# Scores of six head pairs from 64-row operands on the two row halves of TensorE, with the high parts of q and k rounded on ScalarE

## The chip, the cores and the metric

The kernel runs on one core of one Trainium2 chip. A core has TensorE (matmuls; PE in the profile, and PEld for its weight loads), VectorE (DVE), ScalarE (ACT), GpSimd (POOL) and SyncE (SP), which here only issues transfers. The metric is the device time of one execution in microseconds (us). TensorE's granted clock has two levels, 1.2 and 2.4 GHz; the profile shows it as a share of 2.4.

## What is computed

Attention over 16 heads (2 batches of 8) with rotary embedding, then two dense blocks, all in float32:

```python
q_rot, k_rot = rotate(q), rotate(k)            # (2, 8, 576, 64)
scores = q_rot @ k_rot.T / sqrt(64)
attn = exp(scores - max(scores)); attn /= attn.sum(-1) + 1e-9
x = (attn @ v), heads side by side             # (1152, 512)
x = elu(x @ w_in) @ w_out                      # 512 -> 2048 -> 512
x = mish(x @ w2_in) @ w2_out                   # 512 -> 2048 -> 512
```

## The kernel before

Two heads of 64 dimensions make a pair: one head lies on rows (partitions) 0 to 63, the other on 64 to 127. There are eight pairs, p = 0 to 7, called the first to the eighth here. Each tensor that goes into a large product is split into a high part, rounded to the type fp32r that TensorE multiplies fast, and a low part, the rest; a product is the sum of high by high, low by high and high by low.

The work of a pair is cut into nine **units** (TPP = 9), and a hand-written loop over units u = 9 p + i fixes the order of everything on every engine. Units 0 to 7 of a pair are 128 queries of one head each; unit 8 is the 64 left-over queries of both heads together, with block-diagonal tiles bh and bl. In unit u the loop issues, in this order on TensorE: the **score block** of unit u (`do_S`, line 415, into the PSUM tile ps_s of 128 x 2 x 288, one 288-key half in each of its two banks), the **transposes** of the probabilities of unit u - 3 (`do_T`, lines 481 to 486, into psT and psL), and in some units products with v (`do_av`, line 521, into psA, 64 output columns each) or the small products that turn the sums (`do_spread`, lines 458 and 462). VectorE takes the maximum of a score block (mn, line 422), ScalarE the exponential (P, line 435); both move the transposed P out of psT (pt, lines 499 and 501). ScalarE also keeps R, the inverse sums, out of psA (line 466) and rounds the result to XH (line 548); GpSimd or VectorE subtract to get XL (line 552).

`prepare(p, k)` is called in unit k of pair p - 1. With k = 0 it splits k of pair p (`split_half`: GpSimd rounds kh, line 323, and subtracts kl, line 324), with k = 1 it splits q, with k = 2 to 7 GpSimd rotates the pair after that, one step a unit. Between them SyncE issues the transfers that lay the parts out for the score blocks (`stack_k`, `stack_q`). For the first two pairs (FLAT = 2) VectorE and ScalarE split, and nothing is laid out anew except bh and bl.

Two forms of score block stand in the kernel:

- First and second pair: two units at a time, one of each head. Each matmul contracts the 64 rows of its head, so twelve matmuls alternate between rows 0 to 63 and rows 64 to 127.
- Third to eighth pair: transfers stack kh over kl in ka (128 rows) and qh over qh in qa; qb holds ql over zeros. Two matmuls a key half, each on 128 rows, make the three products:

```python
work.append([
    (d["qa"][:, h, cols], lambda ks: d["ka"][:, h, ks]),
    (d["qb"][:, h, cols], lambda ks: d["ka"][:, h, ks]),
])
```

From the seventh pair on, weights of the first dense block are unpacked between the units (`weight_part`): steps of GpSimd and VectorE, then ScalarE's high part and GpSimd's low part. Behind the eighth pair the dense blocks follow.

Of the kernel before, what the change touches and what calls it, by code (L numbers as in the profile page):

```python
# [21 lines left out]
def plain(ap):  # L22
    return ap.bitcast(F32)
# [3 lines left out]
def kernel(  # L27
# [218 lines left out]
    def attention(att, ps, tail):  # L246
# [61 lines left out]
        def split_alloc(p):  # L308
            d = {}
            for nm in ("kh", "kl", "ql"):  # L310
                d[nm] = att.tile([128, S], F32R, tag=nm, name=nm, bufs=2)
            for nm in ("qa",) if p < FLAT else ("ka", "qa"):
                d[nm] = att.tile([128, 2, S], F32R, tag=nm, name=nm, bufs=2)
            d["qh"] = d["qa"][:, 0, :] if p < FLAT else att.tile([128, S], F32R, tag="qh", name="qh", bufs=1)
            i = p % 2
            d["qb"] = qb[i]
            d["bh"], d["bl"] = bd[i]
            sp_t[p] = d

        def split_half(p, i, h, l):  # L320
            d = sp_t[p]
            x = qk_t[p][:, i, :]
            nc.gpsimd.tensor_scalar(out=d[h], in0=x, scalar1=1.0, scalar2=0.0, op0=ALU.mult, op1=ALU.add)
            nc.gpsimd.tensor_tensor(out=d[l], in0=x, in1=plain(d[h]), op=ALU.subtract)
# [24 lines left out]

        def spread(dst, src, r):  # L350
            for h in range(2):
                nc.sync.dma_start(out=plain(dst[64 * r:64 * r + 64, h, :]), in_=plain(src[64 * h:64 * h + 64, :]))

        def stack_k(p):
            d = sp_t[p]
            spread(d["ka"], d["kh"], 0)
            spread(d["ka"], d["kl"], 1)

        def stack_q(p):
            d = sp_t[p]  # L360
            for r in range(0 if p < FLAT else 2):
                spread(d["qa"], d["qh"], r)
            if p >= FLAT:
                spread(d["qb"], d["ql"], 0)
            for r in range(2):
                sl = slice(64 * r, 64 * r + 64)
                nc.sync.dma_start(out=plain(d["bh"][sl, 64 * r:64 * r + 64]), in_=plain(d["qh"][sl, S - 64:S]))
                nc.sync.dma_start(out=plain(d["bl"][sl, 64 * r:64 * r + 64]), in_=plain(d["ql"][sl, S - 64:S]))
# [11 lines left out]
        def do_S(u):  # L380
# [4 lines left out]
            else:  # L385
                us = (u,)
            work = []
            for w in us:
                psS[w] = ps_s()
                if tiles[w % TPP] is None:  # L390
                    work.append([
                        (d["bh"], lambda ks: d["kh"][:, ks]),
                        (d["bh"], lambda ks: d["kl"][:, ks]),
                        (d["bl"], lambda ks: d["kh"][:, ks]),
                    ])
                    continue
                h, t = tiles[w % TPP]
                cols = slice(128 * t, 128 * t + 128)
                if p < FLAT:
                    rows = slice(64 * h, 64 * h + 64)  # L400
                    work.append([
                        (d["qh"][rows, cols], lambda ks, rows=rows: d["kh"][rows, ks]),
                        (d["ql"][rows, cols], lambda ks, rows=rows: d["kh"][rows, ks]),
                        (d["qh"][rows, cols], lambda ks, rows=rows: d["kl"][rows, ks]),
                    ])
                else:
                    work.append([
                        (d["qa"][:, h, cols], lambda ks: d["ka"][:, h, ks]),
                        (d["qb"][:, h, cols], lambda ks: d["ka"][:, h, ks]),
                    ])  # L410
            for a in range(len(work[0]) if work else 0):
                for j in range(2):
                    for w, passes in zip(us, work):
                        l, r = passes[a]
                        nc.tensor.matmul(  # L415
                            psS[w][:, j, :HS], lhsT=l, rhs=r(slice(j * HS, j * HS + HS)),
                            start=(a == 0), stop=(a == len(passes) - 1),
                        )

# [145 lines left out]
        for i in range(2):  # L565
# [5 lines left out]
            bd.append(pair)  # L571
        qb = [att.tile([128, 2, S], F32R, name=f"qb{i}") for i in range(2)]
        for t in sums:
            nc.vector.memset(t[:, :, 1:2], 1e-9)
        nc.vector.memset(pl_t[1][S - 512:128, 256:384], 0.0)
        for t in qb:
            nc.gpsimd.memset(plain(t[64:128]), 0.0)
        nc.gpsimd.memset(halves, 0.0)
# [63 lines left out]
        for u in range(max(av_at) + 1):  # L642
            p, i = divmod(u, TPP)
            for k in range(8):
                if p and i == k and p + 1 < NP:
                    prepare(p + 1, k)
            if u == 2:
# [75 lines left out]
            if u == 1:  # L723
                first_hi(*HEAD[-1])
                nc.scalar.activation(out=tab[:, 0:2, :], in_=tab[:, 2:4, :], func=AF.Copy, scale=QSCALE)
                rope_half(1, 0, nc.gpsimd)
            if u in (5, 6):
                second_split(2 if u == 5 else 0)
# [241 lines left out]
```

## Time and profile before

| | us |
|---|---|
| runs of the kernel: median (lowest to highest) | 559.64 (558.6 to 561.39) |
| profiled execution, first to last instruction | 559.2 |
| TensorE busy in it | 546.1 (98%) |
| VectorE, ScalarE, GpSimd busy | 375.8, 267.4, 244.4 |
| mean granted clock of TensorE, share of 2.4 GHz | 0.994 |

A matmul's row begins when it starts and ends when its results are written, so rows of matmuls that follow each other overlap: what one costs is the distance between starts, not its length. A group of the timeline (x4) reaches from the first start to the last end. What stands in brackets behind a row is the idle time of that engine before it and what ended it; "issue" means that the profile shows nothing that it waited for.

### The profile page before, as it was taken

To read this page: it belongs to the slowest core of one execution; us is meant where nothing else is said; L and a number is where in the kernel's file an instruction comes from. 1 tells how busy PE (TensorE), PEld (TensorE's weight loads), DVE (VectorE), ACT (ScalarE), POOL (GpSimd) and SP (SyncE) were. 2 spreads that over 40 slices of the span, in tenths; PEclk is the share of its full clock that TensorE was granted. 3 is DMA by queue.
4 is the path that set the end of the run, shared out by engine and by line. 5 is a ranking of instruction groups with operands and counts; after the bars stand their busy time and mean duration, and the time that the engine had idled before them with its cause. 6 is when DMAs were issued, how large, how long until landed. Compare 5 with 4: busy or idle time off the path is not lost.

```text
span 559.2 us, 8818 instructions
## 1 busy us (share of the span) xinstructions
PE 546.1 (98%) x3328; PEld 500.5 (90%) x3328; DVE 375.8 (67%) x560; ACT 267.4 (48%) x459; POOL 244.4 (44%) x227
## 2 busy tenths in 40 slices
PE   7889999999999999999999999999999999999997
PEld 6667878888898999999999999999989989989985
DVE  4868777879867888888889878857336555521221
ACT  3746666677656675554554556344342233132120
POOL 7979898953315434434334531534414433310000
PEclk9979999999999999999999999999999999999999
DMA  7379778764331333323232321423222131000012
GB/s 234 106 208 222 184 207 215 198 140 144 88 114 42 113 113 111 112 78 93 96 112 76 114 76 38 139 88 114 84 105 90 62 114 43 34 0 1 38 39 94
DMA packets 49258, 59.82 MB, mean 107 GB/s; under 512 B 20928, under 2 KB 39104, under 8 KB 48448
## 3 DMA queue, kind: packets, MB, share of 16 engines
q1 hardware_dynamic: 48672, 58.67, 35.6%
q8 instruction: 26, 0.43, 0.3%
q10 hardware_dynamic: 544, 0.59, 0.3%
q14 instruction: 16, 0.13, 0.1%
HBM read 47.51 MB, written 2.36 MB: 89 GB/s over the span
## 4 chain that ended last, share of the span: by engine, by line
PE 87%; DVE 3%; POOL 3%; issue 3%; DMA 2%; ACT 1%; SPq 0%; POOLq 0%; ACTq 0%
PE ps_s L187 33%; PE ps_h L801 18%; PE ps_g L777 17%; PE ps_s L415 7%; PE psA L521 7%; PE psT L481 4%; DMA qk_t<-in_qk_dram 1%; DVE mn L422 1%; DMA bh<-qa 1%; ACT P L435 1%; POOL wu L96 1%; POOL wo0bl L127 1%; POOL wo0l L127 1%; PE psL L486 0%; DVE wu L108 0%
## 5 line engine op out<-in xcount | busy, mean ns | idle before, releaser
L100 DVE TENSOR_SCALAR wu<-wu 128x512 int32<-128x512 int32 x64 | 39.7, 620 | 43.1 <-POOL wu L96 43.1
L759 ACT ACTIVATE ta<-ps_s 128x768 f32<-128x768 f32 x24 | 19.5, 812 | 100.8 <-PE ps_s L187 100.8
L422 DVE TENSOR_REDUCE mn<-ps_s 128x1 f32<-128x576 f32 x72 | 53.5, 752 | 21.0 <-PE ps_s L415 20.8
L435 ACT ACTIVATE P<-ps_s,mn 128x576 f32<-128x576 f32 x72 | 53.1, 740 | 14.7 <-DVE mn L422 14.3
L104 DVE SCALAR_TENSOR_TENSOR wu<-raw,wu 128x512 int32<-128x512 int32 x64 | 50.6, 791 | 2.0
L187 PE MATMUL ps_s<-XH,wi0h 128*128 128x384 f32 x192 | 49.1, 336 | 0.0
L108 DVE SCALAR_TENSOR_TENSOR wu<-raw,wu 128x512 int32<-128x512 int32 x64 | 47.8, 747 | 1.8
L187 PE MATMUL ps_s<-XL,wi1h 128*128 128x384 f32 x192 | 48.9, 335 | 0.0
L187 PE MATMUL ps_s<-XL,wi0h 128*128 128x384 f32 x192 | 48.8, 335 | 0.0
L187 PE MATMUL ps_s<-XH,wi1l 128*128 128x384 f32 x192 | 48.8, 335 | 0.0
L187 PE MATMUL ps_s<-XH,wi0l 128*128 128x384 f32 x192 | 48.8, 335 | 0.0
L187 PE MATMUL ps_s<-XH,wi1h 128*128 128x384 f32 x192 | 48.7, 334 | 0.0
L96 POOL TENSOR_SCALAR wu<-raw 128x512 f32<-128x512 f32 x64 | 46.4, 728 | 4.3
L127 POOL TENSOR_TENSOR wi0l<-wu,wi0h 128x512 fp32r<-128x512 f32 x16 | 23.0, 1440 | 57.5 <-ACT wi0h L126 57.5
L127 POOL TENSOR_TENSOR wi1l<-wu,wi1h 128x512 fp32r<-128x512 f32 x16 | 24.3, 1523 | 54.1 <-ACT wi1h L126 54.1
L127 POOL TENSOR_TENSOR wo1l<-wu,wo1h 128x512 fp32r<-128x512 f32 x16 | 23.3, 1462 | 48.6 <-ACT wo1h L126 48.6
L481 PE MATMUL psT<-idn,P 128*128 128x128 f32 x288 | 43.7, 276 | 0.0
L761 DVE TENSOR_TENSOR g<-ta,g 128x768 fp32r<-128x768 f32 x16 | 17.5, 1093 | 37.0 <-ACT g L760 37.0
L501 ACT ACTIVATE pt<-psT 128x512 f32<-128x512 f32 x44 | 26.2, 597 | 28.9 <-PE psT L481 28.9
L521 PE MATMUL psA<-pt,v_t 128*64 128x256 f32 (+1 forms) x240 | 37.1, 410 | 2.3 <-DVE pt L499 1.8
L481 PEld LDWEIGHTS psT<-idn,P 128*128 128x128 f32 x288 | 35.2, 143 | 2.0 <-issue 1.4
L187 PEld LDWEIGHTS ps_s<-XH,wi0h 128*128 128x128 f32 x192 | 34.7, 188 | 1.4 <-issue 0.8
(177 smaller groups left out, 1370.1 us busy)
## 6 DMA issues: line engine op xcount, KB each, us to landing
raw<-in_w_in_dram SPq DMA_DIRECT2D x32, 512.0 KB, 3.7
raw<-in_w_out_dram SPq DMA_DIRECT2D x32, 512.0 KB, 3.2
qk_t<-in_qk_dram SPq DMA_DIRECT2D x6, 1152.0 KB, 5.5
qa<-qh SPq DMA_DIRECT2D x24, 144.0 KB, 2.7
out_dram<-Y SPq DMA_DIRECT2D x9, 256.0 KB, 2.0
ka<-kh SPq DMA_DIRECT2D x12, 144.0 KB, 3.1
ka<-kl SPq DMA_DIRECT2D x12, 144.0 KB, 3.0
qb<-ql SPq DMA_DIRECT2D x12, 144.0 KB, 2.7
```

Of the source, the lines that this page charges most:

```text
L96: nc.gpsimd.tensor_scalar(out=u, in0=high.bitcast(F32), scalar1=REBASE, scalar2=0.0, op0=ALU.mult, op1=ALU.add)
L100: nc.vector.tensor_scalar(out=ui, in0=ui, scalar1=3, scalar2=0x7FFFFFF8, op0=ALU.logical_shift_left, op1=ALU.bitwise_and)
L104: nc.vector.scalar_tensor_tensor(out=ui, in0=high, scalar=-0x80000000, in1=ui, op0=ALU.bitwise_and, op1=ALU.bitwise_or)
L108: nc.vector.scalar_tensor_tensor(out=ui, in0=low, scalar=29, in1=ui, op0=ALU.logical_shift_right, op1=ALU.bitwise_or)
L127: nc.gpsimd.tensor_tensor(out=lo, in0=u, in1=plain(hi), op=ALU.subtract)
L187: nc.tensor.matmul(o[:, j, :CH], lhsT=ws[j][i][:, cc, :], rhs=x[:, cc, t * CH:t * CH + CH], start=(k == 0), stop=(k == 3 * NC - 1),)
L422: nc.vector.tensor_reduce(out=m, in_=psS[u][:, :, :HS], axis=AX.XY, op=ALU.min)
L435: nc.scalar.activation(out=P.rearrange("p (j n) -> p j n", j=2), in_=psS.pop(u)[:, :, :HS], func=AF.Exp, scale=-1.0, bias=mn_t.pop(u), acc ...
L481: nc.tensor.transpose(tv[:, c, :], P[:, k:k + 128], idn)
L521: nc.tensor.matmul(o[64 * h:64 * h + 64, cols], lhsT=v, rhs=rhs, start=(c == 0 and first), stop=(c == 4), skip_group_check=True,)
L777: nc.tensor.matmul(o[:, j, :CH], lhsT=WO[f][w][:, e * 128:e * 128 + 128], rhs=g_part(f, t, i), start=(k == 0), stop=(k == 3 * GF - 1),)
L801: nc.tensor.matmul(o, lhsT=l, rhs=w, start=(k == 0), stop=(k == 3 * GF - 1))
```

## The change

For the third to eighth pair the tiles ka, qa and qb are gone. kx and qx hold the swapped halves: the rows of one head moved to the other half of the partitions, for kx only the half of the keys that is needed there. A score block is now six matmuls on 64 rows: the three products for the first key half from rows 0 to 63, and those for the second from rows 64 to 127, in turn. Of each head one key half comes from the untouched tiles (`native`), the other from kx and qx (`swapped`). The rounding of kh and qh of these pairs moves from GpSimd to ScalarE, and `prepare` moves from the start of a unit to a place behind the unit's exponential. The two clearings of qb at the start fall away.

```diff
         def split_alloc(p):
             d = {}
-            for nm in ("kh", "kl", "ql"):
+            for nm in ("kh", "kl", "qh", "ql"):
                 d[nm] = att.tile([128, S], F32R, tag=nm, name=nm, bufs=2)
...
+            if p >= FLAT:
+                d["qx"] = att.tile([128, 2, S], F32R, tag="qx", name="qx", bufs=2)
+                d["kx"] = att.tile([128, 2, HS], F32R, tag="kx", name="kx", bufs=2)
...
-            nc.gpsimd.tensor_scalar(out=d[h], in0=x, scalar1=1.0, scalar2=0.0, op0=ALU.mult, op1=ALU.add)
+            nc.scalar.activation(out=d[h], in_=x, func=AF.Copy)
             nc.gpsimd.tensor_tensor(out=d[l], in0=x, in1=plain(d[h]), op=ALU.subtract)
...
-        def spread(dst, src, r):
-            for h in range(2):
-                nc.sync.dma_start(out=plain(dst[64 * r:64 * r + 64, h, :]), in_=plain(src[64 * h:64 * h + 64, :]))
+        def swap(dst, src, cut):
+            for r in range(2):
+                c = slice(r * HS, r * HS + HS) if cut else slice(0, S)
+                nc.sync.dma_start(out=plain(dst[64 * r:64 * r + 64]), in_=plain(src[64 - 64 * r:128 - 64 * r, c]))
...
+            def native(nm, n, rows, cs):
+                return d[nm][rows, cs]
+
+            def swapped(nm, n, rows, cs):
+                return d["qx"][rows, n, cs] if nm[0] == "q" else d["kx"][rows, n, :]
+
+            def product(w, j, at, rows, cols):
+                ks = slice(j * HS, j * HS + HS)
+                q, k = [[at(x + y, n, rows, c) for n, y in enumerate("hl")] for x, c in (("q", cols), ("k", ks))]
+                work.append((w, j, ((q[0], k[0]), (q[1], k[0]), (q[0], k[1]))))
...
+                    h, t = tiles[w % TPP]
+                    r = h if p < FLAT else j
+                    product(
+                        w, j, native if r == h else swapped,
+                        slice(64 * r, 64 * r + 64), slice(128 * t, 128 * t + 128),
+                    )
...
-            for k in range(8):
-                if p and i == k and p + 1 < NP:
-                    prepare(p + 1, k)
...
+            if p and i < 8 and p + 1 < NP:
+                prepare(p + 1, i)
```

On TensorE, unit 5 of the third pair stood like this before (L481 and L486 are transposes, L415 the score block):

```order
L481 MATMUL psT_82<-idn,P 128x128 x4
L486 MATMUL psL<-idn,P 128x128
L415 MATMUL ps_s<-ka,qa 128x288 x2
L415 MATMUL ps_s<-ka,qb_118 128x288 x2
L481 MATMUL psT_81<-idn,P 128x128 x4
L521 MATMUL psA<-pt_86,v_t 64x320
```

and stands like this now (the same lines are L479, L484 and L414):

```order
L479 MATMUL psT_82<-idn,P 128x128 x4
L484 MATMUL psL<-idn,P 128x128
L414 MATMUL ps_s<-kx,qx 128x288
L414 MATMUL ps_s<-kh,qh 128x288
L414 MATMUL ps_s<-kx,qx 128x288
L414 MATMUL ps_s<-kh,ql 128x288
L414 MATMUL ps_s<-kx,qx 128x288
L414 MATMUL ps_s<-kl,qh 128x288
L479 MATMUL psT_81<-idn,P 128x128 x4
L519 MATMUL psA<-pt_86,v_t 64x320
```

The neighbours are the same; four matmuls on 128 rows became six that alternate between the untouched and the swapped tiles, so between the two row halves.

On ScalarE, units 0 to 2 of the second pair stood like this before (P is an exponential, pt an evacuation of psT, R the kept inverse sums, XH the rounded result):

```order
L435 ACTIVATE P,sums_78<-ps_s,mn 128x576 x2
L501 ACTIVATE pt_86<-psT_82 128x4x128
L466 ACTIVATE R_407<-psA 128x320
L548 ACTIVATE XH<-R_277 128x256
L435 ACTIVATE P,sums_78<-ps_s,mn 128x576 x2
L501 ACTIVATE pt_85<-psT_81 128x4x128
```

and stand like this now:

```order
L433 ACTIVATE P,sums_78<-ps_s,mn 128x576
L321 ACTIVATE kh<-qk_t 128x576
L433 ACTIVATE P,sums_78<-ps_s,mn 128x576
L499 ACTIVATE pt_86<-psT_82 128x4x128
L464 ACTIVATE R_389<-psA 128x320
L321 ACTIVATE qh<-qk_t 128x576
L546 ACTIVATE XH<-R_273 128x256
L433 ACTIVATE P,sums_78<-ps_s,mn 128x576 x2
```

The copies kh and qh came in, one between the two exponentials and one between R and XH; what stands behind keeps its order.

## Rows read from the trace of the kernel before

**Rows 1.** Busy time of each engine (number of instructions), clock and DMA, 48 to 147 us.
```profile
48.00:147.00 99.00, 98.67 (x803) 81.41 (x803) 79.86 (x159) 69.27 (x168) 69.41 (x62) 1.00 0.71 180
```

**Rows 2.** The matmuls of line 415 with qa: count, duration ns, first and last start.
```profile
L415 PE MATMUL ps_s<-ka,qa x96: 292/340/406, 47.6 to 144.1; 128*128 128x288 f32 x96
```

**Rows 3.** TensorE's timeline (start us, length us), third pair, block between transposes.
```profile
72.98 0.27 PE L486 MATMUL psL<-idn,P 128*128 128x128 f32 x1
73.01 0.51 PE L415 MATMUL ps_s<-ka,qa 128*128 128x288 f32 x2
73.36 0.43 PE L415 MATMUL ps_s<-ka,qb 128*128 128x288 f32 x2
73.63 0.60 PE L481 MATMUL psT<-idn,P 128*128 128x128 f32 x4
```

**Rows 4.** The same timeline in the second pair, a block on 64 rows behind transposes.
```profile
43.00 0.27 PE L486 MATMUL psL<-idn,P 128*128 128x128 f32 x1
43.20 0.54 PE L415 MATMUL ps_s<-kh,qa 64*128 64x288 f32 x4
43.57 0.43 PE L415 MATMUL ps_s<-kh,ql 64*128 64x288 f32 x4
43.83 0.44 PE L415 MATMUL ps_s<-kl,qa 64*128 64x288 f32 x4
44.20 0.44 PE L458 MATMUL psA<-idn,R 128*128 128x128 f32 x2
```

**Rows 5.** The same timeline, second pair, a 64-row block behind the product with v.
```profile
27.01 0.60 PE L521 MATMUL psA<-pl,v_t 128*64 128x256 f32 x4
...
28.52 0.66 PE L481 MATMUL psT<-idn,P 128*128 128x128 f32 x4
```

**Rows 6.** The same timeline, third pair, a block behind the product with v.
```profile
66.32 0.60 PE L521 MATMUL psA<-pl,v_t 128*64 128x256 f32 x4
...
67.49 0.60 PE L481 MATMUL psT<-idn,P 128*128 128x128 f32 x4
```

**Rows 7.** The same timeline, third pair, a block behind the sum product L462.
```profile
69.34 0.33 PE L462 MATMUL psA<-R,halves 128*128 128x64 f32 x2
...
70.14 0.60 PE L481 MATMUL psT<-idn,P 128*128 128x128 f32 x4
70.67 0.48 PE L521 MATMUL psA<-pt,v_t 128*64 128x320 f32 x1
```

**Rows 8.** TensorE's weight loads, the first four of the block of rows 4.
```profile
43.20 0.30 PEld L415 LDWEIGHTS ps_s<-kh,qa 64*128 64x128 f32 x4 [0.17 <-issue]
```

**Rows 9.** ScalarE's copy of a whole k tile: busy us, mean ns | idle before.
```profile
L335 ACT ACTIVATE kh<-qk_t 128x576 fp32r<-128x576 f32 x1 | 0.7, 681 | 0.0
```

**Rows 10.** ScalarE's timeline in the third pair, units 1 and 2.
```profile
68.13 0.60 ACT L501 ACTIVATE pt<-psT 128x512 f32<-128x512 f32 x1 [1.16 <-PE psT L481]
...
69.77 0.44 ACT L466 ACTIVATE R<-psA 128x320 f32<-128x320 f32 x1
```

**Rows 11.** Timelines of ScalarE, GpSimd, VectorE and TensorE, second pair, 31 to 35 us.
```profile
31.76 0.43 ACT L548 ACTIVATE XH<-R 128x256 fp32r<-128x256 f32 x1
...
31.95 1.40 POOL L324 TENSOR_TENSOR kl<-qk_t,kh 128x576 fp32r<-128x576 f32 x1
...
32.22 1.41 DVE L552 TENSOR_TENSOR XL<-R,XH 128x256 fp32r<-128x256 f32 x1 [1.81 <-ACT XH L548]
...
34.58 0.77 PE L521 MATMUL psA<-pt,v_t 128*64 128x320 f32 x1 [1.80 <-DVE pt L499]
```

**Rows 12.** VectorE's timeline at 158 us, GpSimd idle.
```profile
158.11 0.42 DVE L552 TENSOR_TENSOR XL<-R,XH 128x256 fp32r<-128x256 f32 x1
```

**Rows 13.** TensorE's busy time and granted clock (behind the count), 34.5 to 40.5 us.
```profile
34.50:40.50 6.00, 5.92 (x32) 0.51 0.80 193
```

**Rows 14.** TensorE's timeline, two places where it stands idle, seventh pair and later.
```profile
128.23 0.51 PE L521 MATMUL psA<-pt,v_t 128*64 128x256 f32 x2 [0.17 <-ACT R L466]
...
176.69 0.62 PE L777 MATMUL ps_g<-ge,wo0bl 128*128 128x384 f32 x2 [0.81 <-POOL wo0bl L127]
```

More of the change, by code (lines that the diff above doesn't have):

```diff
@@ L309, in split_alloc @@
             d = {}
-            for nm in ("kh", "kl", "ql"):
+            for nm in ("kh", "kl", "qh", "ql"):
                 d[nm] = att.tile([128, S], F32R, tag=nm, name=nm, bufs=2)
[L312 to L317, printed above, removed]
+            if p >= FLAT:
+                d["qx"] = att.tile([128, 2, S], F32R, tag="qx", name="qx", bufs=2)
+                d["kx"] = att.tile([128, 2, HS], F32R, tag="kx", name="kx", bufs=2)
+            d["bh"], d["bl"] = bd[p % 2]
             sp_t[p] = d
@@ L348, in first_lo @@
             )
-        def spread(dst, src, r):
-            for h in range(2):
-                nc.sync.dma_start(out=plain(dst[64 * r:64 * r + 64, h, :]), in_=plain(src[64 * h:64 * h + 64, :]))
+        def swap(dst, src, cut):
+            for r in range(2):
+                c = slice(r * HS, r * HS + HS) if cut else slice(0, S)
+                nc.sync.dma_start(out=plain(dst[64 * r:64 * r + 64]), in_=plain(src[64 - 64 * r:128 - 64 * r, c]))
         def stack_k(p):
             d = sp_t[p]
-            spread(d["ka"], d["kh"], 0)
-            spread(d["ka"], d["kl"], 1)
+            for n, nm in enumerate(("kh", "kl")):
+                swap(d["kx"][:, n, :], d[nm], True)
         def stack_q(p):
             d = sp_t[p]
[L361 to L364, printed above, removed]
+            for n, nm in enumerate(("qh", "ql") if p >= FLAT else ()):
+                swap(d["qx"][:, n, :], d[nm], False)
             for r in range(2):
@@ L388, in do_S @@
             for w in us:
                 psS[w] = ps_s()
[L390 to L410, printed above, removed]
@@ L411, in do_S @@
-            for a in range(len(work[0]) if work else 0):
-                for j in range(2):
[L413 to L418, printed above, removed]
+                for j in range(2):
+                    if tiles[w % TPP] is None:
+                        k = [d[nm][:, j * HS:j * HS + HS] for nm in ("kh", "kl")]
+                        work.append((w, j, ((d["bh"], k[0]), (d["bh"], k[1]), (d["bl"], k[0]))))
+                        continue
+                    h, t = tiles[w % TPP]
[4 more added lines that the diff above has]
+                    )
@@ L420, in do_max @@
+            if p < FLAT:
+                work.sort(key=lambda x: x[1])
+            for a in range(3):
+                for w, j, passes in work:
+                    nc.tensor.matmul(
+                        psS[w][:, j, :HS], lhsT=passes[a][0], rhs=passes[a][1], start=(a == 0), stop=(a == 2),
+                    )
         def do_max(u):
@@ L571, in attention @@
             bd.append(pair)
-        qb = [att.tile([128, 2, S], F32R, name=f"qb{i}") for i in range(2)]
         for t in sums:
@@ L575, in attention @@
         nc.vector.memset(pl_t[1][S - 512:128, 256:384], 0.0)
-        for t in qb:
-            nc.gpsimd.memset(plain(t[64:128]), 0.0)
         nc.gpsimd.memset(halves, 0.0)
```

## The prediction

> **What bounds the kernel now.** I read the busy times by stage first, then TensorE's timeline inside the stage that the change edits, then the instructions of the other engines around the two places where their order moves. In the stretch from 48 to 147 us, in which the scores of the third to eighth pair are made, TensorE is busy 98.67 of 99.00 us, while VectorE, ScalarE and GpSimd have 79.86, 69.27 and 69.41 [rows 1]. So the reader is to see that this stage lasts as long as TensorE's own instructions, and that its price is read from the distances between their starts. The edited instructions are 96 score matmuls with qa there and as many with qb, two and two to a block: 48 blocks, eight in each of six pairs, the first at 47.6 and the last at 144.1 us [rows 2]. The ninth block of a pair (the left-over queries, against bh and bl) stays as it is.
>
> **The score block itself.** Before, a block is four matmuls on all 128 rows. Two of them take 73.63 - 73.36 = 0.27 us, so a slot is 0.13 us [rows 3]. After, it is six matmuls on 64 rows, alternately on rows 0 to 63 and 64 to 127. The trace has this form: the first two pairs already score from 64 rows, in twelve matmuls that alternate in the same way, and there four of them take 43.83 - 43.57 = 0.26 us [rows 4]. Two run side by side in one slot. A block goes from four slots to three: 0.13 us less, 6.3 us over 48 blocks, if nothing else changed.
>
> **What stands around it.** Something else does change: the blocks stand between transposes (of P, L481 and L486), which use all 128 rows. I measure from the last transpose ahead of a block to the first instruction behind it.
> - Now: last transpose 72.98, next transpose 73.63, so 0.65 us, and the four transposes behind take their undisturbed 0.60 us [rows 3].
> - On 64 rows: last transpose 43.00, next instruction 44.20, so 1.20 us with six slots; three slots fewer make 0.81 [rows 4]. The 128-row instructions behind such a block also lose time on their first: four transposes take 0.66 us instead of 0.60 [rows 3, 5]. Together 0.87. A block between transposes thus costs 0.22 us **more**, though its matmuls take 0.13 less: changing the rows in use costs 0.35 us, some 0.17 on the way in (0.20 to the block instead of 0.03 [rows 4, 3]) and 0.18 on the way out.
> - Behind the product with v (L521): that one uses 64 columns, so the way in is dear today too. From its group's start to the transposes behind the block it is now 67.49 - 66.32 = 1.17 us [rows 6]. On 64 rows it is 28.52 - 27.01 = 1.51, less 0.39 for three slots, plus 0.06, so 1.18 [rows 5]. Difference +0.01.
> - Behind the small sum product (L462): now 70.14 - 69.34 = 0.80 [rows 7]. After: 0.06 between its two matmuls, 0.20 to the block, 0.61 for block and way out (44.20 - 43.00 - 0.20 - 0.39), 0.06 behind: 0.93. This row is built up, not seen; +0.13.
>
> Why the way in costs that much stands in the weight loads: the first load for 64 rows begins 0.17 us after the load before it ended, with nothing that it waits for but the sequencer's "issue" [rows 8]. The Trainium skill (TensorE: Matmul & The Clock Gate, Part 2) says that TensorE pulls weight loads ahead of matmuls in flight where the row groups don't conflict or the background weight buffer is the target. By that rule the gap in [rows 8] would not be there and the 48 blocks would give back their whole slot, 6.3 us; the row shows the gap, and I go by the row.
>
> In each of the six pairs four blocks stand behind plain transposes (units 0, 2, 5, 7), one behind the sum product (3) and three behind the product with v (1, 4, 6): 4 x 0.22 + 0.13 + 3 x 0.01 = 1.04 us, and **6.2 us** over six pairs. Bounds: the starts are read to 0.01, a difference to 0.02, so 1.0 us either way over 48 blocks; and the built-up block lies between its two neighbours' 0.01 and 0.22, which is 0.7 less to 0.5 more. So 4.5 to 7.7 us.
>
> **ScalarE's copies.** Twelve copies of 128x576 (high parts of k and q, pairs three to eight) leave GpSimd for ScalarE, where the same copy takes 0.68 us [rows 9]. They stand behind the exponentials of units 0 and 1 of the pair ahead.
> - In the full stage the copy of k falls into 1.16 us in which ScalarE waits for the next transposes: nothing. The copy of q comes just ahead of XH and the keeping of R (69.77, 0.44), which the product with v at 70.67 waits for [rows 10, 7]. Its slack is 0.46 us, so 0.68 would stall it by 0.22; but TensorE comes to it 0.22 + 0.13 later by the sum above, which leaves about nothing. I take 0.05 a pair, **0.3 us**; from 0 to 1.3.
> - In the second pair, between 30 and 35 us, nothing covers them. The chain there runs along ScalarE, two exponentials, an evacuation, R and XH (31.76), then VectorE's XL (32.22), and only behind XL the copy of pt that TensorE waits for, idle 1.80 us until 34.58 [rows 11]. Both copies stand ahead of XH now: 2 x 0.68 = 1.36 us. XL itself took 1.41 us and ended 0.28 us behind GpSimd's kl (31.95 + 1.40); with the copies it would meet ql, which then runs from about 33.45 to 34.87, so XL ends near 35.15 instead of 33.63: 1.5 us. If it met no GpSimd work, XL would take the 0.42 us that it takes at 158 us [rows 12], end at 34.30, and the loss would be 0.7. I take **1.4 us**. From 34.5 to 40.5 TensorE ran at a mean granted clock of 0.51, so nearly all of it at 1.2 GHz, after that idle time [rows 13]. These 6 us cost at most 3 against 2.4 GHz. A stretch half as long again or half as long, after a longer idle time that falls otherwise, is 1.5 us either way. That is in the range, not in the sum.
>
> **What goes for nothing.** GpSimd loses twelve copies and two clearings at the start; it was not the bound, and the first rope waits for its data there. Its subtractions now wait for ScalarE, with XL and the rope steps queued behind; the results are due a pair later, some 10 us off. The transfers of a pair stay ten and fewer bytes go, on SP's queue, between loads that are not due before the next pair. If that cover were gone, the first block of a pair would wait for qx.
>
> **What gives back.** In the seventh and eighth pair TensorE stands idle 0.17 us ahead of the last product with v, until R is kept (128.23 is the first of the two places [rows 14]); TensorE coming 0.22 later takes that up: **-0.3 us**. Behind 147 us the weights' chain makes TensorE wait 0.81 us for GpSimd [rows 14]. That chain is fed through ScalarE and VectorE work on TensorE's own first products, so I let it move with TensorE: 0; at best -0.8. Everything from 177 us on is unchanged.
>
> Sum: 6.2 + 0.3 + 1.4 - 0.3 = **+7.6 us**. On the profiled execution's span of 559.2 that is 566.8; the median of the runs stands 0.4 higher, 559.64, so I predict **567.2 us**.
>
> **Rivals.**
> 1. *The rows change for nothing* (faster). If the distances in [rows 4, 5] came from something particular to the first pairs and blocks on 64 rows entered and left as those on 128 do, each saves its slot: -6.3 + 1.4 = -4.9, 554.7 us. It decides where way in and out together cost under 0.13 us. The Trainium skill (TensorEngine Tiling, Theoretical Speedup) promises up to 2x for a contraction of 64 or less; it would give this case. Against it: the distances agree for two pairs and three kinds of neighbours. 6 in 100.
> 2. *Only the way in costs.* Had the instructions behind a block on 64 rows been late for another reason, 0.18 us a block falls away: 4 x 0.04 - 0.05 - 3 x 0.17 = -0.40 a pair, -2.4, and -2.4 + 0.3 + 1.4 - 0.3 = -1.0: 558.6 us, no change. Against it: transposes and the first product with idn [rows 4, 5] are late alike. 8 in 100.
> 3. *ScalarE becomes the bound.* All twelve copies on the path, ten of them beyond the two counted: +6.8, some 574 us. For it: the thin slack at the product with v. Against it: 29.7 us of ScalarE idle in the stage [rows 1]. 10 in 100.
> 4. *The change doesn't do what it says*: if the halves did not run side by side, six slots instead of three add 0.39 x 48 = 18.7 us, 586 us. 3 in 100.
>
> **How the numbers follow.** The forecast has 73 in 100. About 0.5% (2.8 us) is what a measurement of this kernel can tell from no change: faster 0.06 (rival 1), same 0.08 (rival 2), slower 0.86. The low ends of the forecast are 4.5 + 0 + 0.7 - 0.3 - 0.8 - 1.5 = 2.6, so 562; the high ends 7.7 + 1.3 + 1.5 - 0.3 + 1.5 = 11.7, so 571. I give 561.5 to 571.5; the four rivals, 27 in 100, lie outside, but rival 3 works only in part more often than in full, and such a part falls inside.
>
> **What would show it.** The score blocks of the later pairs: six matmuls in about 0.40 us of slots, but 0.85 to 0.9 us from transpose to transpose against 0.65 now; the first block at about 49.0 us instead of 47.6 and the last at about 151.5 instead of 144.1 [rows 2]. I am wrong if the distance from transpose to transpose is under 0.65, or if TensorE is seen waiting for ScalarE or for qx in the stage.

## The result, and the profile after

The changed kernel takes **567.54 us** (median of 4 runs, 567.26 to 568.56) against 559.12 of the kernel before beside it: a ratio of 1.0144, 95% interval 1.0120 to 1.0169. Run again later, it took 566.63 against 560.06: 1.0128, 1.0109 to 1.0147. It is slower by 6.6 to 8.4 us. The profiled execution after has a span of 566.8 us; that this is the forecast's own figure for the span is chance, since this execution has a stretch at the lowered clock (shown below) that the profiled one of before has not.

[rows 3, 6, 7, 10] stand in the fourth pair and not, as their headings say, in the third: they lie between the ninth blocks at 62.90 and 79.42 us. The pairs from the fourth to the sixth repeat to 0.03 us, so nothing that was read from these rows changes.

The first line has the busy times in the stretch that the edited stage now fills (PE, PEld, VectorE, ScalarE and GpSimd with their instruction counts, then clock and DMA). The second has the matmuls of line 414 from the swapped copies: count, shortest, median and longest duration in ns, first and last start. They answer [rows 1, 2].

```profile
48.00:155.00 107.00, 107.00 (x921) 77.51 (x917) 80.97 (x162) 75.75 (x183) 64.16 (x54) 1.00 0.54 139
```
```profile
L414 PE MATMUL ps_s<-kx,qx x144: 288/292/399, 49.9 to 151.8; 64*128 64x288 f32 x144
```

TensorE is busy all the time in it, and the view of its waits lists none in this stretch. The stage still lasts as long as TensorE's own instructions, but its edited matmuls go from 49.9 to 151.8 us instead of 47.6 to 144.3: 101.9 us instead of 96.7.

TensorE's timeline in the fourth pair (start, length), a block between transposes; it answers [rows 3].

```profile
76.56 0.27 PE L484 MATMUL psL<-idn,P 128*128 128x128 f32 x1
76.77 0.40 PE L414 MATMUL ps_s<-kx,qx 64*128 64x288 f32 x1
76.77 0.40 PE L414 MATMUL ps_s<-kh,qh 64*128 64x288 f32 x1
77.00 0.29 PE L414 MATMUL ps_s<-kx,qx 64*128 64x288 f32 x1
77.01 0.29 PE L414 MATMUL ps_s<-kh,ql 64*128 64x288 f32 x1
77.14 0.29 PE L414 MATMUL ps_s<-kx,qx 64*128 64x288 f32 x1
77.14 0.29 PE L414 MATMUL ps_s<-kl,qh 64*128 64x288 f32 x1
77.36 0.66 PE L479 MATMUL psT<-idn,P 128*128 128x128 f32 x4
```

The six matmuls start in pairs, so they take three slots. But the first pair begins 0.21 us after the last transpose (0.03 in [rows 3]), the transposes behind begin 0.22 after the last pair, and they take 0.66 instead of 0.60. From transpose to transpose it is 0.80 us where it was 0.65.

The same timeline behind the product with v (answers [rows 6]) and behind the sum product (answers [rows 7]); then a weight load behind a block (answers [rows 8], on the way out).

```profile
69.55 0.60 PE L519 MATMUL psA<-pl,v_t 128*64 128x256 f32 x4
...
70.67 0.66 PE L479 MATMUL psT<-idn,P 128*128 128x128 f32 x4
...
72.78 0.33 PE L460 MATMUL psA<-R,halves 128*128 128x64 f32 x2
...
73.64 0.66 PE L479 MATMUL psT<-idn,P 128*128 128x128 f32 x4
74.22 0.48 PE L519 MATMUL psA<-pt,v_t 128*64 128x320 f32 x1
```
```profile
73.64 0.42 PEld L479 LDWEIGHTS psT<-idn,P 128*128 128x128 f32 x4 [0.17 <-issue]
```

The transposes behind each block take 0.66 us instead of 0.60, and that 0.06 is added to the distance here as in the prediction. Behind the product with v the way to the transposes is 1.12 + 0.06 = 1.18 us (1.17 before); behind the sum product 0.86 + 0.06 = 0.92 (0.80). The product with v at 74.22 waits for nothing. The load of a transpose's weights begins 0.17 us late, with nothing but "issue" ahead of it.

The second pair: timelines of ScalarE, GpSimd, VectorE and TensorE, 31 to 37 us; they answer [rows 11].

```profile
31.45 0.67 ACT L321 ACTIVATE kh<-qk_t 128x576 fp32r<-128x576 f32 x1
32.03 0.73 ACT L433 ACTIVATE P<-ps_s,mn 128x576 f32<-128x576 f32 x1
...
33.54 0.70 ACT L321 ACTIVATE qh<-qk_t 128x576 fp32r<-128x576 f32 x1
34.11 0.43 ACT L546 ACTIVATE XH<-R 128x256 fp32r<-128x256 f32 x1
34.31 1.40 POOL L322 TENSOR_TENSOR ql<-qk_t,qh 128x576 fp32r<-128x576 f32 x1 [0.51 <-ACT qh L321]
34.57 1.42 DVE L550 TENSOR_TENSOR XL<-R,XH 128x256 fp32r<-128x256 f32 x1 [2.95 <-ACT XH L546]
...
36.93 0.77 PE L519 MATMUL psA<-pt,v_t 128*64 128x320 f32 x1 [2.39 <-DVE pt L497]
```

Both copies stand ahead of XH, and TensorE waits 2.39 us where it waited 1.80. From one ninth block to the next (25.31 to 48.38 us) this pair lasts 23.07 us instead of 22.13. These are the stretches with the lowered clock (the figure behind GpSimd's count, 0.50); they answer [rows 13]:

```profile
35.50:42.00 6.50, 5.07 (x29) 3.78 (x29) 3.21 (x6) 2.15 (x5) 1.56 (x2) 0.50 0.58 175
```
```profile
11.60:18.40 6.80, 6.42 (x32) 5.53 (x31) 4.21 (x7) 4.59 (x10) 6.64 (x7) 0.50 0.03 5
```

The first of them begins in the longer wait. The other lies in the first pair, ahead of every score block and copy that the change edits; this execution has it and the profiled one of before has not. In the later profile of the changed kernel it is missing too, and the first pair's ninth block starts at 24.01 instead of 25.31 us, so the stretch costs about 1 us. The rest of the kernel only moves: the first L187 starts at 157.12 instead of 149.73, and the wait for the weights is 0.83 us as in [rows 14].

```profile
184.12 0.62 PE L771 MATMUL ps_g<-ge,wo0bl 128*128 128x384 f32 x2 [0.83 <-POOL wo0bl L127]
```

### The profile page after: what moved, and what is told of

The parts are those of the page before. It is cut to its first block, busy times and chain, and to the rows that moved or that the text cites. A ratio compares the mean times of both kernels' runs of the same rounds, so it can differ in the third digit from the quotient of the medians.

```text
span 566.8 us, 8994 instructions
## 1 busy us (share of the span) xinstructions
PE 553.2 (98%) x3424; PEld 495.6 (87%) x3424; DVE 375.1 (66%) x560; ACT 273.7 (48%) x471; POOL 233.7 (41%) x213
## 4 chain that ended last, share of the span: by engine, by line
PE 89%; issue 3%; POOL 3%; DVE 2%; DMA 1%; ACT 1%; SPq 0%; POOLq 0%; ACTq 0%
PE ps_s L187 32%; PE ps_h L795 17%; PE ps_g L771 17%; PE ps_s L414 7%; PE psA L519 7%; PE psT L479 6%; DMA qk_t<-in_qk_dram 1%; ACT P L433 1%; POOL wu L96 1%; POOL wo0bl L127 1%; PE psA L456 1%; PE psL L484 1%; POOL wo0l L127 0%; POOL wi0l L127 0%; DMA v_t<-in_vp_dram 0%
## 5 line engine op out<-in xcount | busy, mean ns | idle before, releaser
L187 PE MATMUL ps_s<-XH,wi0h 128*128 128x384 f32 x192 | 49.1, 336 | 0.0
L187 PE MATMUL ps_s<-XL,wi1h 128*128 128x384 f32 x192 | 48.9, 335 | 0.0
L187 PE MATMUL ps_s<-XL,wi0h 128*128 128x384 f32 x192 | 48.8, 335 | 0.0
L187 PE MATMUL ps_s<-XH,wi1l 128*128 128x384 f32 x192 | 48.8, 335 | 0.0
L187 PE MATMUL ps_s<-XH,wi0l 128*128 128x384 f32 x192 | 48.8, 335 | 0.0
L187 PE MATMUL ps_s<-XH,wi1h 128*128 128x384 f32 x192 | 48.7, 334 | 0.0
L479 PE MATMUL psT<-idn,P 128*128 128x128 f32 x288 | 46.9, 288 | 0.0
L479 PEld LDWEIGHTS psT<-idn,P 128*128 128x128 f32 x288 | 32.3, 144 | 9.9 <-issue 8.0
L187 PEld LDWEIGHTS ps_s<-XH,wi0h 128*128 128x128 f32 x192 | 34.6, 188 | 1.4 <-issue 0.8
```

Source lines behind the costliest of these rows:

```text
L187: nc.tensor.matmul(o[:, j, :CH], lhsT=ws[j][i][:, cc, :], rhs=x[:, cc, t * CH:t * CH + CH], start=(k == 0), stop=(k == 3 * NC - 1),)
L479: nc.tensor.transpose(tv[:, c, :], P[:, k:k + 128], idn)
```

## The experiments

The theory: each visit to 64-row use costs TensorE 0.35 us, against 0.13 that a block saves (stage +5.2); ScalarE's copies cost about 1 us, in the second pair alone. Rivals: the copies lengthen the stage; the halves' overlap hangs on their order; later also, that the clock's part is chance. "Stage" is from the first to the last start of an edited score matmul; the last column counts runs whose mean granted clock is 0.998 or more. That mean is of the whole run. Only one run of each row has a trace, so where the clock of the others fell isn't seen.

| kernel | median us (runs) | before beside it | ratio, 95% interval | stage us | clock 0.998 or more |
|---|---|---|---|---|---|
| after | 567.54 (4) | 559.12 | 1.0144, 1.0120 to 1.0169 | 101.9 | 0 |
| after, again | 566.63 (4) | 560.06 | 1.0128, 1.0109 to 1.0147 | 102.0 | 0 |
| scores only | 565.86 (6) | 559.60 | 1.0094, 1.0063 to 1.0126 | 102.0 | 3 |
| rounding only | 561.94 (12) | 559.60 | 1.0038, 1.0023 to 1.0054 | 97.1 | 0 |
| halves in turn | 567.06 (1) | 559.58 | none | 102.2 | 0 |
| after, three double blocks | 566.91 (6) | 559.60 | 1.0124, 1.0099 to 1.0150 | 100.5 | 0 |
| before, three double blocks | 564.13 (6) | 559.60 | 1.0079, 1.0050 to 1.0108 | 101.0 | 3 |
| after, one double block | 565.07 (5) | 559.58 | 1.0093, 1.0078 to 1.0109 | 99.9 | 0 |
| after, third pair on GpSimd | 565.30 (6) | 559.58 | 1.0104, 1.0086 to 1.0122 | 102.0 | 1 |
| before, long filling | 561.09 (12) | 559.58 | 1.0037, 1.0022 to 1.0053 | 96.6 | 7 |
| after, short filling | 565.27 (5) | 560.06 | 1.0109, 1.0090 to 1.0128 | 101.9 | 4 |
| before, short filling | 559.27 (12) | 560.06 | 0.9990, 0.9977 to 1.0004 | 96.8 | 9 |
| before, later split, short filling | 558.72 (12) | 560.03 | 0.9980, 0.9969 to 0.9991 | 97.0 | 11 |

The kernel before itself has 23 such runs of 68 in the four later sets. With double blocks the last edited block of a pair is issued a unit early, so the stage of the two kernels with three doubles can't be set beside the others; there I compare from ninth block to ninth block.

**One part alone.** The scores are as in the changed kernel, the rounding is on GpSimd at its old place:

```
-            nc.scalar.activation(out=d[h], in_=x, func=AF.Copy)
+            nc.gpsimd.tensor_scalar(out=d[h], in0=x, scalar1=1.0, scalar2=0.0, op0=ALU.mult, op1=ALU.add)
...
+            for k in range(8):
+                if p and i == k and p + 1 < NP:
+                    prepare(p + 1, k)
...
-            if p and i < 8 and p + 1 < NP:
-                prepare(p + 1, i)
```

> Only the score blocks on 64 rows; the high parts of k and q of the third to eighth pair stay with GpSimd, in their old place. Theory (TensorE pays 0.35 us for every change of the rows in use, ScalarE's copies cost only in the second pair): from the first to the last edited score block 101.5 us, as in the changed kernel (96.2 before); the first such block starts where it does before, 47.6 us, up to a clock drop; total 5.3 us above before, 564 to 566. Rival (ScalarE's copies make up part of the longer stage): 99 us or less between the blocks and a total under 563.

The other part alone is the kernel before, with these lines the other way round.

> Only the rounding moved to ScalarE (with its new place behind the exponential); score blocks of four matmuls on 128 rows as before. Theory: the third pair starts 1.1 to 1.5 us later than before, the stage from the first to the last block stays at 96.2 us within 0.4, total 1.1 to 1.5 us above before, about 560.5. Rival (ScalarE becomes the bound of the stage): stage 98 us or more, total 563 or more.

The edited matmuls of the first (kx) and the waits of TensorE in the second pair and in the stage of the other:

```profile
L414 PE MATMUL ps_s<-kx,qx x144: 288/293/399, 47.6 to 149.6; 64*128 64x288 f32 x144
```
```profile
PE psA L521 <- DVE pt L499: 2.4, 1, 2.4
...
PE psA L521 <- ACT R L466: 0.5, 2, 0.3
```

With the scores alone the stage is 102.0 us long, as with both parts: ScalarE's copies cost the new stage nothing, and that rival falls. With the rounding alone it is 97.1 (+0.4, the wait for R grows from 0.3 to 0.5), and the second pair lasts 23.07 us, as with both. The first part is +6.3 us by the medians, the second +2.3: the first lies in the theory's range of 564 to 566, the second misses its 1.1 to 1.5. The clock is mixed into both medians. Like with like, the three runs of the first part with a high clock (median 564.02) stand 5.3 us over the eight such runs of before beside them (558.73), which is the stage's 5.2; the second part, which has no run with a high clock, stands 1.2 over the nine runs of before that have none either (561.93 against 560.70).

**The order of the halves.**

```
-            for a in range(3):
-                for w, j, passes in work:
+            order = [(a, x) for a in range(3) for x in work] if p < FLAT else [(a, x) for x in work for a in range(3)]
+            for a, (w, j, passes) in order:
+                if True:
```

> The changed kernel, with each 64-row score block issued as three products of rows 0 to 63 and then three of rows 64 to 127, not in turns of one and one. If products of the two row halves run beside each other only when they alternate (theory), each of the 48 edited blocks loses about 0.39 us: a block lasts about 1.0 us, the stage gets longer by up to 18.7 us, and the time is about 586 us. If the hardware overlaps them in any order (rival), the time stays at 567 us.

TensorE's timeline of one such block; the program issues the three products of one half (kh, kh, kl), then the three of the other (kx):

```profile
83.25 0.40 PE L415 MATMUL ps_s<-kh,qh 64*128 64x288 f32 x1
83.26 0.40 PE L415 MATMUL ps_s<-kx,qx 64*128 64x288 f32 x1
83.49 0.29 PE L415 MATMUL ps_s<-kh,ql 64*128 64x288 f32 x1
83.50 0.29 PE L415 MATMUL ps_s<-kx,qx 64*128 64x288 f32 x1
...
83.86 0.66 PE L480 MATMUL psT<-idn,P 128*128 128x128 f32 x4
```

They start in pairs all the same, 0.01 us apart. The stage is 0.3 us longer (102.2 against 101.9 and 102.0), not 18.7: my expectation missed, and the rival with its 567 holds, by one run. The Trainium skill (TensorE: Matmul & The Clock Gate, Part 3, The mechanism) says that matmuls start in the order of the program; by the recorded starts this holds within a row half here, and not between the halves, and the trace decides. TensorEngine Tiling (Array Packing), Key Properties, also of the Trainium skill, says that tiles operate independently; that agrees.

**Fewer changes of rows.** The score blocks of units 1 and 2, 4 and 5, 6 and 7 are issued back to back, in the changed kernel and, as a control, in the kernel before:

```
-            if u < NU:
+            if u < NU and not (p >= FLAT and i in (2, 5, 7)):
                 do_S(u)
+                if p >= FLAT and i in (1, 4, 6):
+                    do_S(u + 1)
```

> The changed kernel, but the score blocks of units 1 and 2, 4 and 5, 6 and 7 of the third to eighth pair are issued back to back, with the transposes of both units behind them. Same instructions, three changes of rows in and out fewer in each of six pairs. Theory: 18 x 0.35 = 6.3 us less between the first and the last block, about 95.3 us, and a total of about 561, less what the second block of two now waits for the exponential two units earlier. Rival (a block on 64 rows is dear by itself, wherever it stands): stage and total stay at 101.5 and 567.5.

> The kernel before, with the same blocks back to back; all its score blocks use 128 rows, as the transposes do. Theory: no change of rows is saved, so the stage stays at 96.2 us or grows by waits for the exponentials (up to 1 us), total 559 to 560. Rival (the order of blocks and transposes itself saves time): the same 6 us less as with 64 rows, 553.

Neither time came out (about 561 and 559 to 560 were expected). The new order makes waits of its own: the view of TensorE's waits in the stage, of the changed and then of the earlier kernel in this order,

```profile
PE psA L519 <- ACT R L464: 1.3, 6, 0.3
PE ps_s L414 <- ACT P L433: 0.8, 2, 0.7
```
```profile
PE psA L521 <- ACT R L466: 1.0, 5, 0.2
PE ps_s L415 <- ACT P L435: 0.3, 1, 0.3
```

The kernel before got 0.9 us a pair longer in this order (16.53 to 17.39). The view of waits lists only 0.2 us of that in the fourth pair, because it counts a gap only where no row of a matmul covers it. The starts show more: from the last group of four transposes ahead of the sum product to the transpose behind them it is 0.68 us (69.77 to 70.45) instead of 0.44 (68.57 to 69.01), behind the sum product 0.43 instead of 0.16, and ahead of the pair's last products with v 0.80 instead of 0.53. That makes 0.78 us. The changed kernel has the same three distances, 0.68, 0.43 and 0.80, in this order. So what counts is the difference between the two kernels: +1.00 us a pair with single blocks, -0.10 (17.29 against 17.39) with doubles. That is 1.10 for three changes fewer, where 3 x 0.35 = 1.05 was expected. The agreement is partly luck: such a wait also swallows the price of a change that falls into it (with single blocks the changed kernel had 0.27 behind the sum product and the earlier one 0.16, here both have 0.43). To have it without the new waits, I doubled units 4 and 5 alone:

```
-            if u < NU:
+            if u < NU and not (p >= FLAT and i == 5):
                 do_S(u)
+                if p >= FLAT and i == 4:
+                    do_S(u + 1)
```

> The changed kernel, with only the blocks of units 4 and 5 of each edited pair issued back to back, where the run with three such doubles showed no new wait. Theory (each change of rows in use and back costs 0.35 us): six changes fewer, -2.1 us, an edited stage of about 99.8 us and 565.4 us in all. Rival (the cost belongs to the 64-row blocks, however they are placed): 567.5 us, stage 101.9 us.

TensorE's timeline over such a double in the fourth pair, with its first product, the seam and the transposes behind it:

```profile
73.80 0.40 PE L414 MATMUL ps_s<-kh,qh 64*128 64x288 f32 x1
...
74.17 0.29 PE L414 MATMUL ps_s<-kl,qh 64*128 64x288 f32 x1
74.18 0.42 PE L414 MATMUL ps_s<-kx,qx 64*128 64x288 f32 x2
74.31 0.29 PE L414 MATMUL ps_s<-kh,qh 64*128 64x288 f32 x1
...
74.80 0.66 PE L479 MATMUL psT<-idn,P 128*128 128x128 f32 x4
```

At the seam the second block begins one slot (0.13 us) behind the last products of the first; in and out are paid once. No new wait is listed. The stage is 99.9 us, 2.0 less than after for six changes fewer: **0.33 us for each change of the rows in use and back**. From ninth block to ninth block the fourth to sixth pair last 17.18 us instead of 17.53, which is 0.35; the seventh and eighth save less. The time, 565.07, is near the 565.4 that was expected, and the rival that puts the cost on the blocks themselves falls.

**The copies of the second pair.** Only the third pair's rounding, which runs during the second pair, goes back to GpSimd:

```
-            nc.scalar.activation(out=d[h], in_=x, func=AF.Copy)
+            if p == FLAT:
+                nc.gpsimd.tensor_scalar(out=d[h], in0=x, scalar1=1.0, scalar2=0.0, op0=ALU.mult, op1=ALU.add)
+            else:
+                nc.scalar.activation(out=d[h], in_=x, func=AF.Copy)
```

> The changed kernel, with the third pair's rounding (which runs during the second pair) back on GpSimd at its old place; the fourth to eighth pairs' stay on ScalarE. Theory: the second pair lasts 22.1 us again instead of 23.1 (-0.94), the first edited block starts near 47.6 us plus what an early clock drop adds, and TensorE's wait in the second pair is 1.8 us again instead of 2.4, so that the stretch behind it keeps a granted clock of 1.0 in some of the runs as in the kernel before: 565.5 to 566.5 us. Rival (the copies cost the same in every pair, and the wait has nothing to do with the clock): within 0.3 us of the changed kernel, 567.2 to 567.8 us.

The time, 565.30, is just under the theory's 565.5 to 566.5. But its mean clock rose above 0.997 in one run only, so this doesn't tell the copies' own time from the clock's. In the profiled run the lowered clock lies in the first pair (11.2 to 14.6 us) and not behind the wait. The profiled second pair was shorter than any other, 18.84 us: TensorE waits only 0.94 us, since VectorE's XL took 0.55 us there. XL, and then the busy times and the clock (1.00) from 32 to 42 us:

```profile
32.68 0.55 DVE L553 TENSOR_TENSOR XL<-R,XH 128x256 fp32r<-128x256 f32 x1 [1.80 <-ACT XH L549]
```
```profile
32.00:42.00 10.00, 9.06 (x86) 6.84 (x85) 6.81 (x14) 4.87 (x14) 9.76 (x9) 1.00 0.65 200
```

In all fourteen traces this XL ends 0.28 us behind the instruction with two operands that GpSimd has in hand (here one that ends at 32.95, in [rows 11] kl, in the changed kernel ql). It costs 0.4 us alone [rows 12] and 1.4 where such an instruction has just begun. The Trainium skill (SBUF — State Buffer, Terms) says that VectorE and GpSimd take a shared pair of ports for a whole instruction, the other being blocked; these rows agree.

**The clock.** In the 32 runs of the table that have ScalarE's copies in the second pair and no filling, none reached a mean clock of 0.998; without the copies 30 of 86 did (before, and the three others that round the third pair on GpSimd). The traces agree with the wait as the cause: in all nine in which TensorE stands 1.8 or 2.4 us in this place the clock is lowered behind it, and in none of the other five, with 0.6 to 1.2 us (this last run and the four filled ones below). So I put extra matmuls into the wait, whose result nothing reads. The first try was in the kernel before, ahead of the products with v of the second pair's fourth unit; `keep_warm` is the kernel's own helper, matmuls of a zero tile into psA:

```
+            if u == TPP + 3:
+                keep_warm(14)
```

> The kernel before, with 14 extra matmuls whose result nothing reads, between the transposes of unit 9 and the product with v in the second pair, where TensorE waits 1.8 us and the granted clock then falls. Theory: with the wait filled the clock stays at 1.0 behind it in every run and the time is 557 to 558.5 us in all of them, against a median of 559.6. Rival (the drop does not come from this wait): no change or up to 0.5 us more, with as many runs of a low clock as before.

```profile
33.67 3.36 PE L585 MATMUL psA<-bl 128*128 128x128 f32 x28 [1.15 <-issue]
36.96 0.48 PE L521 MATMUL psA<-pt,v_t 128*64 128x320 f32 x1
```

This missed: the filling begins 1.15 us late, for a reason that the profile doesn't show, takes 3.3 us and so delays the product with v past 34.58 of [rows 11]. The clock was high in 7 of 12 runs, but the kernel is 1.5 us slower. Then I put in shorter ones that wait for nothing, in the changed kernel (8 matmuls) and in the one before (5), beside the changed kernel itself:

```
+            if u == TPP + 3:
+                for _ in range(8):
+                    nc.tensor.matmul(psL[:, 0, :], lhsT=idn, rhs=idn, start=True, stop=True)
```

> The changed kernel itself, once more, beside the next two. Both theories: 567.2 to 567.8 us. If TensorE's wait of 2.4 us in the second pair is what lowers the clock (theory), no run reaches a mean granted clock of 0.998; if the lowered clocks so far were chance (rival), about four runs in ten do, as in the kernel before.

> The changed kernel, with 8 extra matmuls of the identity on itself (16 records of about 0.11 us, 1.8 us) in the second pair's wait of 2.4 us ahead of the product with v; nothing reads their result. Theory (the wait lowers the clock): some runs now reach a mean clock of 0.998 or more, the lowest time falls to 564.5 to 565.5 and the median to 565.5 to 567. Rival (the wait and the clock have nothing to do with each other): 567.2 to 567.8 us, and the clock as in the changed kernel.

> The kernel before, with 5 such extra matmuls (10 records, 1.1 us) in the same wait, 1.8 us there. They fit into the wait, unlike the 3.3 us of the longer filling. Theory: fewer runs with a lowered clock, the best times stay at 558.3 to 558.6 and the median falls from 559.6 to 558.4 to 559.2. Rival (the drop of these runs starts elsewhere): a median of 559.4 to 559.8, spread as before.

TensorE in the second pair, and busy times with the clock (0.50 and 1.00) behind the wait: first of the changed kernel again, then of the changed kernel with the filling.

```profile
35.64 0.76 PE L519 MATMUL psA<-pt,v_t 128*64 128x320 f32 x1 [2.38 <-DVE pt L497]
```
```profile
35.60:39.00 3.40, 3.36 (x17) 2.32 (x17) 1.82 (x3) 1.55 (x4) 0.00 (x0) 0.50 0.66 179
```
```profile
33.49 1.95 PE L688 MATMUL psL<-idn 128*128 128x128 f32 x16
36.03 0.45 PE L519 MATMUL psA<-pt,v_t 128*64 128x320 f32 x1 [0.59 <-DVE pt L497]
```
```profile
33.00:41.00 8.00, 7.41 (x68) 6.11 (x69) 5.84 (x11) 3.60 (x10) 1.91 (x2) 1.00 0.74 221
```

Without the filling TensorE runs at 1.2 GHz from 35.6 to 39.0 us, behind the wait; with it, at 2.4 GHz throughout. Four of five runs now reach 0.998, against none of four, and the median falls by 1.4 us to 565.27 with the same stage, as the theory said. (The changed kernel beside it, 566.63, is below both theories' 567.2; its clock, 0.994 to 0.997, is above the 0.988 to 0.994 of its first runs, with the same stage.) In the kernel before, 9 of 12 runs have the high clock instead of 6 of 17 beside them. Its median falls by 0.8, to 559.27, between the two expectations, and a ratio of 0.9990 (0.9977 to 1.0004) can't be told from none. So the clock behind this wait costs the changed kernel 1.4 us; how much of that the kernel before pays as well, 0.8 by its median or nothing, isn't settled.

**A version that may beat both.** This is the kernel before with three such matmuls, and with the calls that prepare a pair moved to the end of the step as in the changed kernel; the rounding is left on GpSimd:

```
-            for k in range(8):
-                if p and i == k and p + 1 < NP:
-                    prepare(p + 1, k)
...
+            if u == TPP + 3:
+                for _ in range(3):
+                    nc.tensor.matmul(psL[:, 0, :], lhsT=idn, rhs=idn, start=True, stop=True)
...
+            if p and i < 8 and p + 1 < NP:
+                prepare(p + 1, i)
```

> The kernel before, with the calls that prepare the next pair at the end of a step (as in the changed kernel, but all rounding on GpSimd), and 3 extra matmuls (6 records, 0.65 us) in the second pair's wait. In the run with the third pair's rounding on GpSimd at the end of a step, the XL of the second pair took 0.55 us, between two of GpSimd's differences, and not 1.41 beside one. If the place in the step does that (theory), XL takes about 0.5 us, the second pair lasts 18.8 to 19.3 us at a full clock and the time is 557.3 to 558.6 us, against 559.6 to 560.1 of the kernel before. If it was the chance of that one run (rival), XL takes 1.4 us again, the second pair lasts 19.8 us at a full clock, and the time is that of the shorter filling, 559.0 to 559.5 us.

```profile
32.04 1.41 DVE L552 TENSOR_TENSOR XL<-R,XH 128x256 fp32r<-128x256 f32 x1 [1.80 <-ACT XH L548]
```

The place was not it: XL takes 1.41 us again and the second pair 19.8, as the rival says. What sets GpSimd's instructions against XL in one run and not in another stays open; the one trace with the short XL also has the lowered clock in the first pair, and whether that shifts them isn't shown. The clock was high in 11 of 12 runs, though, and **558.72 us**, 0.9980 (0.9969 to 0.9991), between the two expectations, is the lowest median of all kernels here. It has two edits at once, so how much the moved calls add to the filling wasn't separated.

## Why the prediction was right

It said 567.2 us and +7.6; measured were 566.6 and 567.5, +6.6 and +8.4. Step by step:

1. **The slots.** Three instead of four, as read from [rows 3, 4]. Right.
2. **Changing the rows in use.** Between transposes +0.22 was said and 0.21 came; behind the product with v +0.01 and +0.01; behind the sum product, which was built up, +0.13 and +0.12. A pair: 1.04 said, 17.53 - 16.53 = 1.00 measured between the ninth blocks of the third and fourth pair. The price of a change and back, 0.35, is 0.33 by the double block's stage and 0.35 by its pairs. The Trainium skill (TensorE: Matmul & The Clock Gate, Part 2) has weight loads pulled ahead under two conditions, and the prediction read it as making the way in free. At these places no load is pulled ahead: a gap as in [rows 8] is there on the way out too, 0.17 us. Whether the skill's conditions are met there isn't seen.
3. **What gives back.** -0.3 said. Before, the seventh and the eighth pair took 16.83 and 17.00 us, 0.3 and 0.5 more than the others; after, 17.61 each, 0.1 more. So about 0.6 came back: this term was sized too small, since I had counted only the 0.17 that the view lists for each of the two waits for R. Steps 2 and 3 together: 5.9 said, 5.2 measured over the stage.
4. **ScalarE's copies in the stage.** 0.3 said, nothing measured (scores alone and both parts: 102.0 and 101.9 us).
5. **The copies in the second pair.** 1.4 said. The mechanism was right: XL meets ql and takes 1.42 us, and TensorE waits for pt behind it. (The branch in which XL meets nothing was added up wrongly: 32.22 + 1.36 + 0.42 is 34.00 and not 34.30, a loss of 0.4 instead of 0.7. It only lowers the range's low end by 0.3.) The size was not: a copy of 0.68 us delays the next instruction by 0.57 or 0.58 (31.45 to 32.03, 33.54 to 34.11), since that one starts before the copy's record ends. Two make 1.15. In the profiles at full clock the pair lasts 20.94 us (after, filled) against 19.81 (before, filled): 1.13.
6. **The clock.** Left out of the sum, at 1.5 us either way in the range. This step failed, inside a forecast that came true: I took the drop for something that both kernels have and asked only how long it lasts. In the traces that have it, it costs the second pair 2.3 us before (22.13 against 19.81 with the filling) and 1.3 or 2.1 after (22.23 and 23.07 against 20.94), so it doesn't get dearer. What differs is how often it comes: by the count above the kernel before escapes it in a third of its runs, and the changed one, with the longer wait, in none.

So the terms that are seen make 5.2 + 1.1 = 6.3 us, 1.3 under the sum. Runs with a high clock bear that out: 565.20, the median of the four with the filling, against 558.81, that of the six of before beside them, is 6.4. What the medians have above it, 0.2 us in the second comparison and 2.0 in the first, is the clock's share by this reckoning. It stood in the range and not in the sum, so that 7.6 lies between the measured 6.6 and 8.4 is in part luck: the terms of the sum came out too large together, and one was missing. The difference of 0.4 us between median and span was misread as well: each run's time is about 1.8 us over its own span (568.56 and 566.8), so the profiled execution of before, with 559.2, was one of about 561, a long one of its kind. As the sum was in effect added to the median of 559.64, this cost nothing.

Of the rivals, the free change of rows (554.7) and the way in alone (558.6) fall by the rows above, ScalarE as the bound (574) by the scores alone, and halves that don't run side by side (586) by the pairs of starts.

## What to carry to other kernels

Packing two 64-row products side by side saves a slot (0.13 us a block here), but each visit between 128-row work has an entry and an exit price on TensorE (0.33 us here, so by these numbers, as an estimate, three blocks a visit before it pays; no run here has three). Behind a product that changes the columns in use anyway a block cost only 0.01 more than before. So count visits and their neighbours, and not matmuls. A move of work to an idle engine is judged at the place with the least slack, here the second pair, not by the engine's share. A wait that gets longer ahead of dense work can cost more than its length, through the clock (1.4 us here); compare the clock over many runs, not in one profile. A full busy share doesn't mean that nothing is lost: the 0.24 us between two groups of transposes above stand in no list of waits, so measure from start to start.

## What the runs showed that I had not expected

- The two row halves pair up whether the program alternates them or issues one behind the other: 102.2 against 101.9 us of stage.
- The lowered clock is a matter of odds, and they shift with the wait: a high mean clock in 30 of 86 runs without ScalarE's copies in the second pair (the wait is 1.8 us in three of their four traces, 0.94 in the other), in 0 of 32 with the copies and a wait of 2.4 us, in 31 of 41 with the wait partly filled by matmuls that nobody reads (all four filled kernels together).
